# Weight conversions at even distances, their first steps pinned to the order of emission

## The chip, the cores and the metric

The kernel runs on one core of a Trainium2 chip. The time is the device time of one execution in microseconds (us); three executions of the kernel before were timed, and one more was profiled. Engines are called as the profile calls them: PE is TensorE (PEld its weight loads), DVE is VectorE, ACT is ScalarE, POOL is GpSimd, SP is SyncE, whose queue issues all the DMAs here.

## The reference

A block of local and global attention is followed by two feed-forward networks, all in float32:

```python
s_ll = where(|i - j| <= 32, q_l @ k_l.T / 8, -1e9);  s_lg = q_l @ k_g.T / 8
out_l = softmax([s_lg, s_ll]) @ [v_g, v_l];  out_g = softmax(q_g @ [k_g, k_l].T / 8) @ [v_g, v_l]
x = concat(out_g, out_l)                  # 2176 tokens (4 batches of 544), 512 wide
x = relu(x @ w_in) ** 2 @ w_out           # 512 -> 2048 -> 512
out = ((x @ w1) * (x @ w2)) @ w3 @ w_out2 # 512 -> 1024 -> 1024 -> 512
```

## The kernel before

**Products of split numbers.** A float32 factor is held as two parts, `hi` (rounded) and `lo` (the rest), and a product is three matmuls (`PASSES`). Activations are split in tiles named `hl`: ACT rounds (L460, or L471 in `h_unit`), DVE subtracts (L106).

**Weights.** The 72 weight tiles w0 to w71 of 128 x 512 come as 8-byte words and are converted on the chip. `load_w(n)` loads tile `wraw` (512 KB, two buffers). `conv_a(n)`: ACT, two steps (L415, L416). `conv_b(n)`: DVE, two steps (L421, then L424), and the load of w(n+2). `conv_c(n)`: POOL adds (L434), ACT rounds into the final tile (L435), DVE subtracts (L106). The final tiles are named by their pool tag: `va` for w16 to w23, `vb` for w24 to w31, `ub` for w32 to w39, `ua` for w40 to w63, `ub` for w64 to w71. `conv(n)` emits conv_c(n-1), conv_b(n) and conv_a(n+1).

**Stages.** Pass A takes each of eight token blocks (256 or 288 columns) through the first half of the first network, interleaved with the attention; its last two blocks (6 and 7, from about 345 us) run after the attention, as lists of steps made by `rows`: `h_unit` f = 0 to 7 (12 matmuls, relu and squares on ACT L470, L475, L471, a DVE split into `hl`), and `x_add` f (12 matmuls into `acc`), which needs that split. Pass B (from about 398 us) does the same for eight blocks with w16 to w31; x_add f needs w(24+f). In pass B the sixteen `w_unit`s multiply w3 by the last weights (12 matmuls of 512 columns into `wacc`, L652): unit u needs w32 to w39 and w(40+u). Each second unit is copied by ACT to tile `ws` (L658) and stored; `ws` shares the two `wraw` buffers. The last stage (from about 652 us) needs w56 to w71 and the stored products.

**Order.** `merge(main, (steps, lo, hi))` runs the main list and emits the steps of a fill list spread over main steps lo to hi. The framework's scheduler then sets the order on each engine by its own estimate of the times: an instruction that it holds ready is placed ahead of earlier-emitted ones that are not. `tc.keep_in_program_order(ins)` adds one edge: ins stands behind the instruction emitted just before it on the same engine. On the chip each engine keeps the order that is set.

Of the kernel before, what the change touches and what calls it, by code (L numbers as in the profile page):

```python
# [9 lines left out]
F32 = mybir.dt.float32  # L10
# [4 lines left out]
AF = mybir.ActivationFunctionType  # L15
# [49 lines left out]
RUNS = (0, 16, len(UNITS))  # L65
# [10 lines left out]
def attention_mlp(ctx: ExitStack, tc: tile.TileContext, kq0, kq, vw, wts, mask, ident, out):  # L76
    nc = tc.nc
# [329 lines left out]
    def load_w(n):  # L407
        t = pools["cv"].tile([128, 512, 2], I32, tag="wraw", name="wraw", bufs=2)
        nc.sync.dma_start(out=t, in_=wts[n].bitcast(I32).rearrange("p (c w) -> p c w", w=2))
        raw_t[n] = t  # L410

    def conv_a(n):
        raw = raw_t[n]
        t = [pools["cv"].tile([128, 512], I32, tag=f"wt{k}", name="wt", bufs=2) for k in range(3)]
        nc.scalar.activation(t[0].bitcast(F32), raw[:, :, 1].bitcast(F32), AF.Copy, scale=2.0**-112)  # L415
        nc.scalar.activation(t[2], raw[:, :, 0].bitcast(U32), AF.Copy, scale=2.0**-29)  # L416
        mid_t[n] = t

    def conv_b(n):
        raw, (a, b, _) = raw_t.pop(n), mid_t[n]  # L420
        nc.vector.tensor_scalar(  # L421
            out=a, in0=a, scalar1=3, scalar2=0x7FFFFFF8, op0=ALU.logical_shift_left, op1=ALU.bitwise_and
        )
        nc.vector.scalar_tensor_tensor(  # L424
            out=b, in0=raw[:, :, 1], scalar=-(1 << 31), in1=a, op0=ALU.bitwise_and, op1=ALU.bitwise_or
        )
        if n + 1 not in RUNS and n + 2 not in RUNS:
            load_w(n + 2)

    def conv_c(n):  # L430
        _, b, m = mid_t.pop(n)
        tag = UNITS[n]
        t = pools[tag].tile([128, 2, 512], F32R, tag=tag, name=tag, bufs=8)
        nc.gpsimd.tensor_tensor(out=b, in0=b, in1=m, op=ALU.add)  # L434
        nc.scalar.copy(t[:, 0], b.bitcast(F32))  # L435
        split_lo(nc.vector, t[:, 1], b.bitcast(F32), t[:, 0])
        w_t[n] = t

    def conv(n):

        if n in RUNS:
            conv_a(n)
        else:
            conv_c(n - 1)
        conv_b(n)
        if n + 1 in RUNS:
            conv_c(n)
        else:
            conv_a(n + 1)
# [59 lines left out]
    def rows(i, w_in, w_out, split, end):  # L509

        n = block(i)[1]
        steps = []
        for f in range(9):
            if f < 8:
                steps.append(lambda f=f: h_unit(i, f, w_in + f))
            if 4 <= f < 8:
                steps.append(lambda f=f: split(f - 4))
            if f > 0:
                steps.append(lambda f=f: x_add(i, f - 1, w_t[w_out + f - 1], n))
        steps.append(lambda: [end(d) for d in range(4)])  # L520
        return steps
# [5 lines left out]
    def merge(main, *fills):  # L527

        at = [0] * len(fills)
        for n, f in enumerate(main):  # L530
            f()
            for k, (steps, lo, hi) in enumerate(fills):
                upto = min(len(steps), max(0, -(-len(steps) * (n + 1 - lo) // (hi - lo))))
                while at[k] < upto:
                    steps[at[k]]()
                    at[k] += 1
        assert all(a == len(f[0]) for a, f in zip(at, fills))
# [39 lines left out]
    main = [lambda f=f: h_unit(0, f, f) for f in range(8)]  # L577
# [8 lines left out]
    def split_a(i, d):  # L586
        if i < NBLK:
            split_x(i, d, xcols(i)[:, d])
        else:
            split_x(i, d, x_t[0][:, 0, d])  # L590
# [12 lines left out]
    for i in range(0, NBLK, 2):  # L603
        main = []
        for j in (i, i + 1):
            if j >= SHARED:
                main += rows(
                    j, 0, 8, lambda d, j=j: split_a(j + 1, d), lambda d, j=j: end_a(j, d, acc[d])
                )
                continue  # L610
            if j > 0:
                main += [lambda f=f, j=j: h_unit(j, f, f) for f in range(8)]
            main += [lambda d=d, j=j: x_unit_a(j, d) for d in range(4)]
        b = i // 2 + 1
        if b < B:
            if b == 1:
                spill(1)
                load_kq(H // 2)
                for k in range(H, min(H + 3, FIRST_SPLIT)):
                    load_v(k)  # L620
            if b * H == FIRST_SPLIT:
                at_cm.__exit__(None, None, None)
                cv_cm.__exit__(None, None, None)
                at_cm, cv_cm = pool("at2", "right"), pool("sp")
                at, pools["cv"] = at_cm.__enter__(), cv_cm.__enter__()
                for k in range(2):
                    load_v(FIRST_SPLIT + k)
            steps = [s for j in range(4 * b - 1, 4 * b + 4) for s in cycle(j, j < 4 * b + 3, j >= 4 * b)]
            steps.append(lambda i=i: (spill(i + 2), spill(i + 3)))
            fills = [(steps, 0, len(main) - 5)]  # L630
        else:
            for cm in (at_cm, rot_cm, cv_cm):
                cm.__exit__(None, None, None)
            u2 = pools["va"] = pools["vb"] = ctx.enter_context(pool("u2", "right"))
            pools["cv"] = ctx.enter_context(pool("cv2"))
            load_w(16)
            load_w(17)
            main.insert(18, lambda: load_x(0))
            fills = [([lambda n=n: conv(n) for n in range(16, 33)], 0, 31)]
        merge(main, *fills)  # L640


# [2 lines left out]
    def w_unit(f, half):  # L645
        if half == 0:
            wacc[f] = ps.tile([128, 512], F32, tag="x", name="wacc", bufs=X_BUFS)
        o = wacc[f]
        w3 = w_t[40 + 2 * f + half]
        for q in range(4):  # L650
            for k, (a, b) in enumerate(PASSES):
                mm(  # L652
                    o, w3[:, a, 128 * q : 128 * (q + 1)], w_t[32 + 4 * half + q][:, b],
                    start=(half + q + k == 0), stop=(half + q + k == 6),
                )
        if half == 1:
            t = pools["cv"].tile([128, 512], F32, tag="wraw", name="ws", bufs=2)
            nc.scalar.copy(t, o)  # L658
            nc.sync.dma_start(out=w_d[f], in_=t)
# [12 lines left out]
    main = []  # L672
    for i in range(NBLK):
        main += rows(
            NBLK + i, 16, 24, lambda d, i=i: split_b(i + 1, d), lambda d, i=i: end_b(i, d)
        )
    fill = [lambda n=n: conv(n) for n in range(33, 43)]
    for f in range(8):
        fill.append(lambda f=f: w_unit(f, 0))
        fill.append(lambda f=f: w_unit(f, 1))  # L680
        if f < 7:
            fill += [lambda n=n: conv(n) for n in (43 + 2 * f, 44 + 2 * f)]
    fill += [lambda n=n: conv(n) for n in range(57, 72)]
    merge(main, (fill, len(main) // 10, 9 * len(main) // 10))

# [131 lines left out]
```

## Time and profile before

| | us |
|---|---|
| median of 3 executions | 945.86 (944.57 to 948.61) |
| the profiled execution | 945.08 |
| its span, first to last instruction | 943.3 |
| PE busy | 899.1 |
| ACT, DVE, POOL busy | 499.5, 469.6, 321.2 |

PE is the engine with the most work. What a change can give here is read from PE's idle time in the stage concerned, and from what ends it.

### The profile page before, as it was taken

What the parts mean: (1) busy time and instruction counts of PE and PEld (TensorE: products, weight loads), DVE (VectorE), ACT (ScalarE), POOL (GpSimd) and SP (SyncE); (2) the same over time, 40 slices, a digit from 0 to 9 for tenths busy, and PEclk for the clock granted to TensorE, in tenths of its full rate; (3) what the DMA queues carried; (4) which work ended last, traced back from release to release, by engine and by line L of the source; (5) the groups of instructions that cost most, each with busy time, mean ns of one, the idle gap of its engine ahead of it and who ended that gap; (6) DMA issues with size and microseconds to landing.
All of it is one profiled execution on the core that took longest, in us unless ns stands there. A gap on an engine that the chain in (4) does not pass through costs nothing.

```text
span 943.3 us, 16424 instructions
## 1 busy us (share of the span) xinstructions
PE 899.1 (95%) x6064; PEld 822.3 (87%) x6064; DVE 469.6 (50%) x1139; ACT 499.5 (53%) x1291; POOL 321.2 (34%) x354
## 2 busy tenths in 40 slices
PE   7899899799999999988999999999999999999998
PEld 4677798699999989987999999999988888888886
DVE  6984465466867649999354353994110210200201
ACT  6975767657667748887464464884211211211211
POOL 5593452376656824433011121430211111111111
PEclk9999999989999999999999999999999999999999
DMA  8644667665668335656144333654200110100101
GB/s 269 204 148 115 168 156 186 184 142 127 156 188 200 84 108 172 227 178 202 32 157 146 132 112 134 207 192 133 98 23 1 43 42 1 42 1 1 42 1 42
DMA packets 61952, 113.07 MB, mean 120 GB/s; under 512 B 6320, under 2 KB 37168, under 8 KB 61872
## 3 DMA queue, kind: packets, MB, share of 16 engines
q1 hardware_dynamic: 61872, 112.03, 40.3%
q8 instruction: 48, 0.79, 0.3%
q14 instruction: 32, 0.26, 0.1%
HBM read 71.63 MB, written 19.92 MB: 97 GB/s over the span
## 4 chain that ended last, share of the span: by engine, by line
PE 63%; DMA 12%; DVE 10%; ACT 4%; issue 4%; POOL 4%; SPq 3%; DVEq 0%; POOLq 0%; ACTq 0%
PE ab L110 20%; PE acc L504 16%; PE h L110 9%; PE wacc L652 5%; PE x L110 4%; DMA wraw<-in_wts 4%; PE o L339 4%; DMA kq_hl<-kqhi 3%; PE sc L110 2%; DMA kqraw<-in_kq 2%; DVE wt L421 2%; DVE wt L424 2%; PE tp L305 2%; DVE hl L106 2%; POOL wt L434 1%
## 5 line engine op out<-in xcount | busy, mean ns | idle before, releaser
L434 POOL TENSOR_TENSOR wt<-wt 128x512 int32<-128x512 int32 x72 | 101.5, 1409 | 232.8 <-DVE wt L424 158.3
L723 DVE TENSOR_TENSOR r<-r,ab 128x480 f32<-128x480 f32 (+1 forms) x40 | 24.3, 607 | 220.2 <-PE ab L110 219.5
L110 PE MATMUL h<-hl,ua 128*128 128x256 f32 (+1 forms) x768 | 121.3, 303 | 8.5 <-ACT r L470 6.1
L110 PEld LDWEIGHTS h<-hl,ua 128*128 128x128 f32 x768 | 107.7, 200 | 12.4 <-ACT r L470 7.0
L504 PE MATMUL acc<-hl,vb 128*128 128x256 f32 (+1 forms) x768 | 112.9, 290 | 5.2 <-DVE hl L106 4.9
L110 PE MATMUL h<-hl,va 128*128 128x256 f32 (+1 forms) x768 | 112.3, 288 | 1.9 <-DVE hl L106 1.9
L106 POOL TENSOR_TENSOR hl_c<-r,hl_c 128x480 fp32r<-128x480 f32 x32 | 39.2, 1224 | 210.8 <-ACT hl_c L725 203.0
L504 PEld LDWEIGHTS acc<-hl,vb 128*128 128x128 f32 x768 | 103.0, 188 | 9.0 <-DVE hl L106 7.3
L110 PEld LDWEIGHTS h<-hl,va 128*128 128x128 f32 x768 | 102.9, 188 | 3.7 <-DVE hl L106 2.8
L110 PE MATMUL x<-hl,ub 128*128 128x288 f32 (+1 forms) x576 | 88.8, 295 | 3.3 <-POOL hl L106 3.3
L504 PE MATMUL acc<-hl_c,wv 128*128 128x480 f32 x384 | 89.2, 380 | 0.0
L110 PE MATMUL ab<-hl_c,ua 128*128 128x480 f32 x384 | 87.1, 380 | 0.0
L110 PE MATMUL ab<-hl_c,ub 128*128 128x480 f32 x384 | 86.6, 380 | 0.0
L110 PEld LDWEIGHTS ab<-hl_c,ub 128*128 128x128 f32 x384 | 72.0, 188 | 11.9
L722 ACT COPY r<-ab 128x480 f32<-128x480 f32 (+1 forms) x40 | 20.9, 522 | 116.1 <-PE ab L110 113.8
L110 PEld LDWEIGHTS ab<-hl_c,ua 128*128 128x128 f32 x384 | 71.9, 188 | 11.9
L110 PEld LDWEIGHTS x<-hl,ub 128*128 128x128 f32 x576 | 76.8, 189 | 6.1 <-POOL hl L106 4.5
L504 PEld LDWEIGHTS acc<-hl_c,wv 128*128 128x128 f32 x384 | 72.0, 188 | 11.4
L204 ACT ACTIVATE p<-p,st 128x256 f32<-128x256 f32 x128 | 64.2, 504 | 22.5 <-DVE st L200 22.3
L214 POOL TENSOR_TENSOR p<-p,st 128x512 f32<-128x512 f32 x56 | 61.8, 1106 | 35.4 <-DVE st L209 27.6
L470 ACT ACTIVATE r<-h 128x288 f32<-128x288 f32 (+1 forms) x128 | 49.2, 391 | 43.9 <-PE h L110 43.3
L415 ACT ACTIVATE wt<-wraw 128x512 f32<-128x512 f32 x72 | 48.4, 672 | 34.9 <-DMA wraw<-in_wts 32.4
(108 smaller groups left out, 1554.7 us busy)
## 6 DMA issues: line engine op xcount, KB each, us to landing
wraw<-in_wts SPq DMA_DIRECT2D x72, 512.0 KB, 3.4
kq_hl<-kqhi SPq DMA_DIRECT2D x24, 280.0 KB, 3.2
kq_hl<-kqraw SPq DMA_DIRECT2D x48, 136.0 KB, 3.2
vraw<-in_vw SPq DMA_DIRECT2D x16, 256.0 KB, 3.3
x2l<-x_d SPq DMA_DIRECT2D x4, 960.0 KB, 6.0
out<-y SPq DMA_DIRECT2D x16, 240.0 KB, 2.3
kqraw<-in_kq SPq DMA_DIRECT2D x24, 144.0 KB, 2.9
kq_hl<-kqraw SPq DMA_DIRECT2D x24, 144.0 KB, 3.4
```

Source lines behind the costliest of these rows:

```text
L106: eng.tensor_tensor(out=lo, in0=raw, in1=hi.bitcast(F32), op=ALU.subtract)
L110: mm(o, w, x, start=(k == 0), stop=(k == len(terms) - 1))
L204: nc.scalar.activation(p[:, n, :], p[:, n, :], AF.Exp, bias=least[:, n : n + 1], scale=-1.0, accum_out=sums[:, n, 0:1],)
L214: nc.gpsimd.tensor_tensor(out=p, in0=p, in1=over.unsqueeze(2).to_broadcast([128, 2, 256]), op=ALU.mult)
L339: mm(to, w, x, start=(k == 0), stop=(k == len(terms) - 1))
L415: nc.scalar.activation(t[0].bitcast(F32), raw[:, :, 1].bitcast(F32), AF.Copy, scale=2.0**-112)
L434: nc.gpsimd.tensor_tensor(out=b, in0=b, in1=m, op=ALU.add)
L470: nc.scalar.activation(r, h, AF.Relu)
L504: mm(acc[d], w[:, a, 128 * d : 128 * (d + 1)], g_t[f][:, b], start=(f + k == 0), stop=(f + k == 9),)
L652: mm(o, w3[:, a, 128 * q : 128 * (q + 1)], w_t[32 + 4 * half + q][:, b], start=(half + q + k == 0), stop=(half + q + k == 6),)
L722: nc.scalar.copy(r, a)
L723: nc.vector.tensor_tensor(out=r, in0=r, in1=b, op=ALU.mult)
```

## The change

The conversions of w16 to w71 are spread differently, and two of their instructions (L415 and L421 of before) get the edge. In the last main list of pass A there were 17 conversions in 31 of 43 steps, now 14 over all 43. In pass B there were 55 entries from step 16 to 151 of 168, with w_units two by two; now 4 conversions stand in the first 12 steps, and 38 entries from step 12 to 154, of which sixteen hold a conversion and, right behind it, the w_unit that uses the tile before.

```diff
-        nc.scalar.activation(t[0].bitcast(F32), raw[:, :, 1].bitcast(F32), AF.Copy, scale=2.0**-112)
+        first = nc.scalar.activation(t[0].bitcast(F32), raw[:, :, 1].bitcast(F32), AF.Copy, scale=2.0**-112)
+        if n >= RUNS[1]:
+            tc.keep_in_program_order(first)
...
-        nc.vector.tensor_scalar(
+        first = nc.vector.tensor_scalar(
...
+        if n >= RUNS[1]:
+            tc.keep_in_program_order(first)
...
-            fills = [([lambda n=n: conv(n) for n in range(16, 33)], 0, 31)]
+            fills = [([lambda n=n: conv(n) for n in range(16, 30)], 0, len(main))]
...
-    fill = [lambda n=n: conv(n) for n in range(33, 43)]
-    for f in range(8):
-        fill.append(lambda f=f: w_unit(f, 0))
-        fill.append(lambda f=f: w_unit(f, 1))
-        if f < 7:
-            fill += [lambda n=n: conv(n) for n in (43 + 2 * f, 44 + 2 * f)]
-    fill += [lambda n=n: conv(n) for n in range(57, 72)]
-    merge(main, (fill, len(main) // 10, 9 * len(main) // 10))
+    late = [lambda n=n: conv(n) for n in range(30, 34)]
+    fill = [lambda n=n: conv(n) for n in range(34, 72)]
+
+    for u in range(16):
+        fill[u + 7] = lambda u=u: (conv(41 + u), w_unit(u // 2, u % 2))
+    merge(main, (late, 0, 12), (fill, 12, 11 * len(main) // 12))
```

The first place is DVE at the start of the stretch, at the conversions of w16 to w18. In the order of before:

```order
L421 TENSOR_SCALAR wt_4853<-wt_4853 128x512
L424 SCALAR_TENSOR_TENSOR wt_4854<-wraw_4830,wt_4853 128x512
L421 TENSOR_SCALAR wt_4862<-wt_4862 128x512
L424 SCALAR_TENSOR_TENSOR wt_4863<-wraw_4832,wt_4862 128x512
L106 TENSOR_TENSOR hl_4848<-r_4847,hl_4848 128x256
L106 TENSOR_TENSOR va_4886<-wt_4854,va_4886 128x512
L106 TENSOR_TENSOR hl_4881<-r_4880,hl_4881 128x256
L106 TENSOR_TENSOR va_4934<-wt_4863,va_4934 128x512
```

And in the changed kernel, whose lines L423, L428 are L421, L424 of before:

```order
L106 TENSOR_TENSOR hl_4848<-r_4847,hl_4848 128x256
L423 TENSOR_SCALAR wt_4853<-wt_4853 128x512
L428 SCALAR_TENSOR_TENSOR wt_4854<-wraw_4830,wt_4853 128x512
L106 TENSOR_TENSOR hl_4881<-r_4880,hl_4881 128x256
L106 TENSOR_TENSOR hl_4916<-r_4915,hl_4916 128x256
L106 TENSOR_TENSOR va_4921<-wt_4854,va_4921 128x512
L423 TENSOR_SCALAR wt_4862<-wt_4862 128x512
L428 SCALAR_TENSOR_TENSOR wt_4863<-wraw_4832,wt_4862 128x512
L106 TENSOR_TENSOR hl_4960<-r_4959,hl_4960 128x256
L106 TENSOR_TENSOR hl_5009<-xb_3756,hl_5009 128x288
L106 TENSOR_TENSOR hl_5004<-r_5003,hl_5004 128x256
L106 TENSOR_TENSOR va_4977<-wt_4863,va_4977 128x512
```

Before, the first DVE step of a conversion stood ahead of the last one of the conversion before it; now it stands behind it, and the splits of activations (`hl`) stand in between.

The second place is ACT where the same conversions begin. Before:

```order
L415 ACTIVATE wt_4853<-wraw_4830 128x512
L416 ACTIVATE wt_4855<-wraw_4830 128x512
L470 ACTIVATE r_4847<-h_4834 128x256
L415 ACTIVATE wt_4862<-wraw_4832 128x512
L471 ACTIVATE hl_4848<-r_4847 128x256
```

And now (L418 is L416 of before, L474, L475, L479 are L470, L471, L475):

```order
L418 ACTIVATE wt_4855<-wraw_4830 128x512
L474 ACTIVATE r_4847<-h_4834 128x256
L475 ACTIVATE hl_4848<-r_4847 128x256
L479 ACTIVATE r_4847<-r_4847 128x256
L415 ACTIVATE wt_4853<-wraw_4830 128x512
```

Only the pinned step moved behind the first relu; the other one still stands ahead of it.

The third place is PE and ACT among the w_units. Before, PE took the two units of one product in one go, from tiles that DVE had finished well ahead (ua_6563 stands 23 rows before ua_6591 in DVE's order):

```order
L652 MATMUL wacc_6638<-ub_5839,ua_6563 128x512 x3
L652 MATMUL wacc_6638<-ub_5867,ua_6563 128x512 x3
L652 MATMUL wacc_6638<-ub_5901,ua_6563 128x512 x3
L652 MATMUL wacc_6638<-ub_5968,ua_6563 128x512 x3
L504 MATMUL acc_6344<-hl_6558,vb_5407 128x256
L504 MATMUL acc_6348<-hl_6558,vb_5407 128x256
L504 MATMUL acc_6352<-hl_6558,vb_5407 128x256
L504 MATMUL acc_6356<-hl_6558,vb_5407 128x256
L652 MATMUL wacc_6638<-ub_6012,ua_6591 128x512 x3
```

Now a unit comes after each 12 matmuls of the main list, each from the tile that was converted last (L508, L656 are L504, L652 of before):

```order
L656 MATMUL wacc_6545<-ub_5752,ua_6532 128x512 x2
L110 MATMUL h_6826<-hl_6495,va_5071 128x288 x2
L656 MATMUL wacc_6545<-ub_5752,ua_6532 128x512
L656 MATMUL wacc_6545<-ub_5799,ua_6532 128x512 x3
L656 MATMUL wacc_6545<-ub_5846,ua_6532 128x512 x3
L656 MATMUL wacc_6545<-ub_5905,ua_6532 128x512 x3
L110 MATMUL h_6826<-hl_6529,va_5071 128x288 x3
L110 MATMUL h_6826<-hl_6589,va_5071 128x288 x3
L110 MATMUL h_6826<-hl_6651,va_5071 128x288 x3
L508 MATMUL acc_6779<-hl_6809,vb_5423 128x288
L656 MATMUL wacc_6545<-ub_5981,ua_6592 128x512 x2
```

ACT there has the first steps of two conversions, the copy to `ws` (L662, L658 of before) and the rounding (L439, L435 of before) behind each other:

```order
L415 ACTIVATE wt_6475<-wraw_6385 128x512
L418 ACTIVATE wt_6477<-wraw_6385 128x512
L479 ACTIVATE r_6808<-r_6808 128x288
L415 ACTIVATE wt_6540<-wraw_6473 128x512
L418 ACTIVATE wt_6542<-wraw_6473 128x512
L662 COPY ws_6492<-wacc_6392 128x512
L439 CAST ua_6592<-wt_6476 128x512
L474 ACTIVATE r_6839<-h_6826 128x288
L439 CAST ua_6666<-wt_6541 128x512
```

Before, the copy stood ahead of the next conversion's first steps, with the steps of two h_units and no other conversion around it.

## Rows read from the trace of the kernel before

**Rows 1.** Busy time of each engine by stretches, from 345 us on.

```profile
core 0: us, PE busy (x) PEld busy (x) DVE busy (x) ACT busy (x) POOL busy (x), PEclk, DMA share, GB/s
345.00:400.00 55.00, 50.10 (x378) 48.99 (x377) 45.77 (x69) 42.65 (x100) 20.04 (x15) 0.97 0.66 216
400.00:440.00 40.00, 34.20 (x259) 32.20 (x259) 38.49 (x55) 32.63 (x76) 15.79 (x12) 1.00 0.50 167
440.00:580.00 140.00, 140.00 (x969) 132.53 (x968) 66.97 (x120) 75.51 (x173) 22.73 (x17) 1.00 0.41 135
580.00:652.00 72.00, 69.29 (x519) 66.85 (x518) 51.24 (x84) 52.18 (x120) 18.98 (x13) 1.00 0.49 161
652.00:943.30 291.30, 286.97 (x1452) 251.31 (x1452) 45.03 (x76) 57.41 (x111) 45.14 (x40) 1.00 0.09 32
```

**Rows 2.** PE's waits from 345 to 440 us: total, times, longest.

```profile
PE acc L504 <- DVE hl L106: 6.3, 8, 1.4
PE h L110 <- ACT r L470: 2.8, 2, 2.1
PE h L110 <- DVE hl L106: 1.5, 2, 1.0
```

**Rows 3.** PE's largest wait from 580 to 655 us, columns as above.

```profile
PE acc L504 <- DVE hl L106: 1.9, 4, 0.9
```

**Rows 4.** Groups on DVE and POOL, 345 to 440 us: busy, mean ns, idle before.

```profile
L424 DVE SCALAR_TENSOR_TENSOR wt<-wraw,wt 128x512 int32<-128x512 int32 x26 | 18.0, 692 | 0.9
L421 DVE TENSOR_SCALAR wt<-wt 128x512 int32<-128x512 int32 x26 | 13.8, 533 | 9.6 <-ACT wt L415 9.6
L106 DVE TENSOR_TENSOR ub<-wt,ub 128x512 fp32r<-128x512 f32 x8 | 12.8, 1598 | 0.1
...
L434 POOL TENSOR_TENSOR wt<-wt 128x512 int32<-128x512 int32 x26 | 35.8, 1378 | 66.7 <-DVE wt L424 55.8 <-ACT hl L471 4.3 <-ACT r L470 3.0
```

**Rows 5.** Timeline at 372 us: start, duration, engine, line.

```profile
372.70 1.34 POOL L434 TENSOR_TENSOR wt<-wt 128x512 int32<-128x512 int32 x1 [2.12 <-ACT va L435]
...
372.82 1.78 DVE L106 TENSOR_TENSOR va<-wt,va 128x512 fp32r<-128x512 f32 x1
```

**Rows 6.** Timeline of one conversion without overlap, 543.8 to 547.8 us.

```profile
543.80 0.43 DVE L421 TENSOR_SCALAR wt<-wt 128x512 int32<-128x512 int32 x1 [3.41 <-ACT wt L415]
...
544.26 0.69 DVE L424 SCALAR_TENSOR_TENSOR wt<-wraw,wt 128x512 int32<-128x512 int32 x1
...
545.12 1.29 POOL L434 TENSOR_TENSOR wt<-wt 128x512 int32<-128x512 int32 x1 [16.14 <-ACT hl L471]
...
545.58 1.12 DVE L106 TENSOR_TENSOR hl<-r,hl 128x256 fp32r<-128x256 f32 x1 [0.63 <-ACT r L475]
546.45 0.62 ACT L435 CAST ua<-wt 128x512 fp32r<-128x512 f32 x1 [0.90 <-POOL wt L434]
...
547.10 0.69 DVE L106 TENSOR_TENSOR ua<-wt,ua 128x512 fp32r<-128x512 f32 x1 [0.40 <-ACT ua L435]
...
547.71 0.43 DVE L421 TENSOR_SCALAR wt<-wt 128x512 int32<-128x512 int32 x1
```

**Rows 7.** Chain that ended last, 550 to 600 us: start, us, what.

```profile
555.47 1.42 PE acc L504 x12
...
558.31 2.75 PE wacc L652 x12
...
578.59 1.59 PE acc L504 x12
...
586.18 0.60 ACT ws L658
...
586.79 2.01 DMA w_d<-ws
...
588.82 4.06 DMA wraw<-in_wts
```

**Rows 8.** Timeline of ACT, then of PE, 347 to 354 us.

```profile
350.96 0.66 ACT L415 ACTIVATE wt<-wraw 128x512 f32<-128x512 f32 x1 [2.63 <-DMA wraw<-in_wts]
351.52 0.65 ACT L416 ACTIVATE wt<-wraw 128x512 int32<-128x512 uint32 x1
352.08 0.37 ACT L470 ACTIVATE r<-h 128x256 f32<-128x256 f32 x1
352.35 0.69 ACT L415 ACTIVATE wt<-wraw 128x512 f32<-128x512 f32 x1
...
352.50 1.68 PE L110 MATMUL h<-hl,ua 128*128 128x256 f32 x12 [2.13 <-ACT r L470]
```

**Rows 9.** DMA issues, 345 to 652 us: KB each, median us to landing.

```profile
wraw<-in_wts SPq DMA_DIRECT2D x56, 512.0 KB, 3.3
```

## The prediction

> **What bounds the kernel now.** Start with the busy time by stretches [rows 1]: the change touches only what is converted from 345 us on, so what PE loses there is all that can come back. PE is idle for 4.9 us from 345 to 400 us, 5.8 from 400 to 440, none from 440 to 580, 2.7 from 580 to 652: 13.4 us. Behind 652 us no conversion is left, and its 4.3 us are at the end. The granted clock is 1.00 or close to it (0.97 in the first stretch, 1.00 in the others), so no term here is one of clock. Next the waits: of the 10.7 us before 440 us, 7.8 end with a DVE split of an activation and 2.8 with a relu on ACT [rows 2]; the late idle time is mostly DVE again [rows 3].
>
> DVE is what is full there: busy 38.5 of 40 us, but 67 of 140 in the next stretch, where PE never waits [rows 1]. In 95 us it ran 26 conversions [rows 4], one each 3.7 us, ten of them of w32 and later, which no block of tokens needs. The groups show an oddity: the last DVE step of a conversion took 1.6 us on average for `ub` [rows 4], and 1.78 us where it began beside a POOL add [rows 5], against 0.69 us alone [rows 6]. A conversion so takes up to 0.4 + 0.7 + 1.8 = 2.9 us of a queue that also holds the splits PE waits for. The kernel before thus converts in two bursts, each with PE idle, and coasts in between.
>
> **What the change does.** The work is the same: 72 conversions, the same splits and loads. Only places change, so the sum is one of idle time, stretch by stretch.
>
> First the new pace. The pin puts a conversion's first DVE step behind the last DVE step of the one before, so conversions no longer overlap; each costs a full chain: DVE, DVE, POOL, ACT, DVE. The trace holds this chain with nothing in its way: L421 at 543.80, L424, the add at 545.12, the rounding at 546.45, the split at 547.10, the next L421 at 547.71 us [rows 6], 3.9 us. In the changed order 17 other DVE steps of some 0.43 us stand between L421 and L424 in the 40 conversions of w16 to w55, 0.2 us each; and the rounding can find ACT, four fifths busy in the full stretch [rows 1], at another step, for which I add 0.2 to 0.3. I take 4.3 to 4.4 us per conversion; 3.9 is the floor, and 5.3 (the chain plus two whole ACT steps of 0.7) the ceiling.
>
> Against it stands what PE has to do meanwhile. From the first matmul that needs w26 to the first that needs w51, the changed order gives PE 303 matmuls of 256 columns, 360 of 288 and 132 of 512. At 1.42, 1.59 and 2.75 us per 12 [rows 7] these are 35.9 + 47.7 + 30.3 = 113.8 us for 25 conversions, 4.55 each. Among the w_units it is tighter: 12 matmuls of 512 and 12 of 288 per conversion, 4.34 us. So the chain just fits, with little to spare. The gains and losses:
>
> - Start, 2.1 of the 4.9 us. PE waited from 350.4 for a relu that stood behind L415 and L416, both waiting for the first load until 350.96 [rows 8]. Only L415 moves behind it, and L416 still waits for that load; the relu comes one step of 0.56 us earlier. 1.6 stay. (Had both moved, the relu would wait for no load.)
> - The rest to 400 us, 2.8 us. About as many conversions run here as before, but each holds DVE for 1.8 us instead of up to 2.9, since the add of a conversion falls between its own DVE steps. Bounds 0 and 2.8; the steps behind a waiting split still wait with it, so I keep half, 1.4.
> - 400 to 440 us, 5.8 us. Here PE's order asks for w26 to w31 themselves, one per 4.6 us, and the chain gives one per 4.4. Bounds 0 and 5.8; nearer to the first, as the pace fits: 1.5.
> - 440 to 580 us, nothing lost so far. The work taken out of the burst now lies here. What stands against it is the buffer that `ws` shares with `wraw`. For a pair of conversions it goes round: load 3.3 us [rows 9], the second load's first steps some 1.4 behind (two loads issued together fed ACT at 350.96 and 352.35 [rows 8]), 1.1 for those two steps, copy 0.6, store 2.0 [rows 7]: 8.4 us, or 9.2 with the load of 4.06 that stood in the chain [rows 7]. PE has 2 x 4.34 = 8.7 us. Over seven pairs that is 0 to 3.5 us; I take 1.5, and 0.5 for chance encounters between w32 and w39.
> - 580 to 652 us, 2.7 us. The last fifteen conversions had 2.5 blocks of pass B and now have 3, some 5 us each; 1.0 stays, the more so as in the last block DVE now has one split of a stored product ahead of the first activation split. Bounds 0 and 2.7.
>
> The loads move with L424, which issues them, and SP's queue keeps the order loads and stores had; a load has one chain of 3.9 us to land in 3.3, so it stays covered, and the cover is gone if a load takes over 5 us.
>
> Idle after: 1.6 + 1.4 + 1.5 + 2.0 + 1.0 = 7.5 us instead of 13.4. The gain is 5.9 us: 945.08 - 5.9 = 939.2 for the profiled execution, which lies 0.8 under the median shown, so 940.0 for a median.
>
> One row speaks against the change. In the chain alone, the activation split beside the POOL add took 1.12 us instead of some 0.42 [rows 6]. In the new order such splits stand right there, one to three per conversion, where before the conversion's own split took most of the hit. If PE had no slack, 24 conversions (w16 to w39) at 0.7 us would cost 17 us; but in the stretch from 440 to 580, where these rows lie, PE lost nothing with 17 adds [rows 1]. I charge nothing beyond the terms above. The Trainium skill, SBUF — State Buffer, section Who interferes with whom, states the rule: a DVE instruction with two SBUF inputs and a GpSimd instruction that reads SBUF exclude each other, and the second to start waits for the whole of the first. By that rule a split that starts with the add loses its full 1.3 us, and the 24 would cost at most 31 us in all without slack, none with it; the trace agrees with the size (1.78 against 0.69).
>
> **Rivals.**
>
> *Slower: the chain becomes the bound.* If the rounding or a load is late often enough, a conversion takes over 4.55 us, and PE, which now uses each tile right after it is made, waits for each. At 5.2 us: 25 x 0.65 = 16 us, idle 1.6 + 1.4 + 16 + 1.0 = 20 us, 7 more than before, 953. It breaks even at 4.9 us and is slower by over 0.5% from 5.1 on. For it: ACT is about four fifths busy where the pins begin, and no step behind one that waits for a load can pass it. Against it: the bare chain leaves 0.65 us, and conversions that are fewer per microsecond leave ACT freer.
>
> *No change that can be seen: the waits move.* DVE still serves in order, and now a waiting split holds the activation splits behind it, where before a busy one did. If that costs what the fullness cost, PE loses 11 to 14 us as before: 943 to 947. For it: three quarters of the waiting is for splits in that queue [rows 2]. Against it: DVE is busy for 1 us less per conversion.
>
> *All of it comes back.* With conversions spread evenly, DVE would be busy everywhere as it is from 440 to 580 us, where PE lost nothing [rows 1]. Only the first stall stays: 13.4 - 1.6 = 11.8 us, 934. Against it: the pace in the first 60 us hardly falls. The Trainium skill, Perfetto Trace Analysis, section Optimization Strategy, gives this as advice: where the most-contended engine changes over time, interleaving those regimes may improve performance; no run here shows it yet for this kernel.
>
> **How the numbers follow.** The forecast gets 0.52, with a range of its own from 936.5 to 943; the chain as bound 0.17; waits that move 0.18; all back 0.13. A difference of 0.5%, 4.7 us, is about what a measurement of this kernel can tell from none. Four fifths of the forecast's range lie below 941.1: 0.42, and with "all back" 0.55 for faster. Of the chain's 0.17, 0.11 is beyond 950.6. The rest, 0.34, is within. The range from 935.5 to 947 leaves out the far half of "all back" and most of the chain's case, a fifth together.
>
> **What would show it.** Right: L421 at least 3.9 us apart from 350 us on, nowhere a conversion's last split of 1.7 us, DVE below nine tenths from 400 to 440 us, PE idle there under 3 us, and a first stall of 1.6 us at 350 us. Wrong: PE waits on `acc` for `vb` or on `wacc` for `ua`, distances of L421 of 5 us and more between w26 and w56, ACT idle before L415 for loads by more than 2 us at a time, or PE idle from 440 to 580 us above 4 us.

## The result, and the profile after

The changed kernel took 932.71 us (median of four executions), the kernel before 945.23 beside it on the same chip: a ratio of 0.985, 95% interval 0.982 to 0.988. It is faster by 12.5 us where 5.9 were forecast, and lies below the range. One of the four, the profiled one, ran at a granted clock of 0.848 and took 977.42 us, so the ratio is of the other three (median 932.52), and the rows here are of a second set of executions of the same kernel. That set has a median of 934.46 us (ratio 0.989, 0.986 to 0.993); its profiled execution took 933.09, with a span of 931.3.

Busy time by stretches, answering to [rows 1]:

```profile
core 0: us, PE busy (x) PEld busy (x) DVE busy (x) ACT busy (x) POOL busy (x), PEclk, DMA share, GB/s
345.00:400.00 55.00, 53.03 (x426) 52.63 (x424) 29.88 (x59) 38.67 (x93) 12.91 (x10) 1.00 0.52 169
400.00:440.00 40.00, 39.83 (x319) 39.62 (x318) 25.82 (x51) 31.14 (x76) 10.40 (x9) 1.00 0.49 165
440.00:580.00 140.00, 138.69 (x934) 128.90 (x933) 78.53 (x147) 88.85 (x197) 37.88 (x29) 1.00 0.52 174
580.00:652.00 72.00, 71.10 (x561) 70.22 (x560) 45.10 (x87) 49.64 (x118) 13.95 (x12) 1.00 0.47 154
652.00:931.30 279.30, 274.95 (x1353) 239.34 (x1351) 38.14 (x59) 51.96 (x96) 43.20 (x38) 1.00 0.07 24
```

PE's idle time is now 2.0, 0.2, 1.3 and 0.9 us in the four stretches, 4.4 in all instead of 13.4. From 400 to 440 us DVE is busy for 25.8 of 40 us instead of 38.5, and PE does 319 matmuls there instead of 259. PE's waits in the windows 345 to 440, 440 to 580 and 580 to 655 us (total, times, longest), answering to [rows 2, 3]:

```profile
PE h L110 <- ACT r L474: 2.1, 3, 1.6
...
PE acc L508 <- DVE hl L106: 0.9, 2, 0.7
PE h L110 <- ACT r L474: 0.4, 1, 0.4
...
PE h L110 <- ACT r L474: 0.8, 1, 0.8
```

The 7.8 us that ended with a DVE split before 440 us are gone altogether. The groups of 345 to 440 us (busy, mean ns, idle before), answering to [rows 4]:

```profile
L438 POOL TENSOR_TENSOR wt<-wt 128x512 int32<-128x512 int32 x18 | 23.3, 1295 | 75.7 <-DVE wt L428 56.4 <-ACT wt L418 11.6 <-ACT hl L475 4.9
L428 DVE SCALAR_TENSOR_TENSOR wt<-wraw,wt 128x512 int32<-128x512 int32 x19 | 13.1, 688 | 0.4
L423 DVE TENSOR_SCALAR wt<-wt 128x512 int32<-128x512 int32 x19 | 8.0, 420 | 0.1
L106 DVE TENSOR_TENSOR vb<-wt,vb 128x512 fp32r<-128x512 f32 x8 | 5.5, 691 | 4.3 <-ACT vb L439 4.1
```

Nineteen conversions run there instead of 26, and the last split takes 0.69 us each time, not up to 1.78 [rows 5]. The timeline from 348 us shows the first stop and the first conversion, answering to [rows 6, 8]:

```profile
348.73 2.63 PE L110 MATMUL h<-hl,ua 128*128 128x256 f32 x21
...
351.99 0.66 ACT L418 ACTIVATE wt<-wraw 128x512 int32<-128x512 uint32 x1 [2.67 <-DMA wraw<-in_wts]
352.56 0.37 ACT L474 ACTIVATE r<-h 128x256 f32<-128x256 f32 x1
...
352.98 1.68 PE L110 MATMUL h<-hl,ua 128*128 128x256 f32 x12 [1.62 <-ACT r L474]
...
354.41 0.43 DVE L423 TENSOR_SCALAR wt<-wt 128x512 int32<-128x512 int32 x1
...
354.87 0.69 DVE L428 SCALAR_TENSOR_TENSOR wt<-wraw,wt 128x512 int32<-128x512 int32 x1
...
355.73 1.30 POOL L438 TENSOR_TENSOR wt<-wt 128x512 int32<-128x512 int32 x1 [18.30 <-DVE wt L428]
...
357.17 0.62 ACT L439 CAST va<-wt 128x512 fp32r<-128x512 f32 x1
...
357.82 0.69 DVE L106 TENSOR_TENSOR va<-wt,va 128x512 fp32r<-128x512 f32 x1
...
358.43 0.42 DVE L423 TENSOR_SCALAR wt<-wt 128x512 int32<-128x512 int32 x1
```

The first stop lasts 1.62 us, since the relu L474 still stands behind L418, which waits for the first load. A conversion takes 4.0 us and the next begins when its split is done; the add (355.73 to 357.03) meets no last split.

**A stage to compare by.** What lies ahead of 345 us is not touched by the change, and yet the first `h` matmul of block 6 began anywhere from 345.5 to 350.2 us in the profiles that are compared here, though PE, DVE, ACT and POOL have the same instructions in the same order up to there. The runs are therefore also compared by the stage from that matmul to the first `ab` matmul of the last stage. Its busy time before, and in the changed kernel:

```profile
347.74:652.47 304.73, 291.32 (x2103) 278.31 (x2102) 202.33 (x325) 203.23 (x467) 77.54 (x56) 0.99 0.48 159
```

```profile
348.73:640.39 291.66, 287.31 (x2103) 276.02 (x2102) 171.92 (x325) 202.21 (x467) 73.18 (x56) 1.00 0.50 166
```

The columns are those of the first fence. The stage is 13.1 us shorter (the span 12.0, as it began 1.0 later). PE's idle time fell by 9.1 us, from 13.4 to 4.3; the other 4.0 came out of its busy time, 291.3 to 287.3 us for the same matmuls. PE has 957 matmuls of 256 columns, 952 of 288 and 192 of 512 here; at the pace of [rows 7] they need 113.2 + 126.1 + 44.0 = 283 us. So the stage before had lost 21 us and not 13.4.

Part of the 4.0 is clock. The mean of 0.97 in the first stretch of [rows 1] is a granted clock of 0.50 (1.2 GHz) for 3.41 us and of 1.00 (2.4 GHz) for the rest:

```profile
372.17:375.58 3.41, 3.41 (x17) 3.41 (x17) 3.38 (x6) 3.34 (x8) 1.34 (x1) 0.50 0.44 156
```

There 16 matmuls, eight of 256 and eight of 288 columns, took 3.54 us from start to start (372.10 to 375.64), for which the pace of [rows 7] gives 2.0: 1.5 us are lost, and PE counts as busy. In the changed kernel the clock stays at 1.00 for the whole stage. The other 2.5 us lay in stops: the first 0.16 us of each do not show as idle time (the last section), and the stage before has 21 stops that show, the changed one 8.

### The profile page after: what moved, and what is told of

Its sections match the earlier page's. It is cut to its first block, busy times and chain, and to the rows that moved or that the text cites. A ratio compares the mean times of both kernels' runs of the same rounds, so it can differ in the third digit from the quotient of the medians.

```text
span 975.6 us, 16410 instructions
## 1 busy us (share of the span) xinstructions
PE 945.8 (97%) x6064; PEld 853.8 (88%) x6064; DVE 441.0 (45%) x1139; ACT 501.4 (51%) x1291; POOL 315.9 (32%) x354
## 4 chain that ended last, share of the span: by engine, by line
PE 83%; DMA 7%; ACT 3%; DVE 3%; SPq 2%; POOL 2%; issue 1%; DVEq 0%; POOLq 0%; ACTq 0%
PE acc L508 24%; PE ab L110 21%; PE h L110 18%; PE x L110 5%; PE wacc L656 5%; PE o L339 4%; DMA wraw<-in_wts 3%; PE sc L110 2%; PE tp L305 2%; DMA kq_hl<-kqhi 2%; DMA kqraw<-in_kq 1%; DMA vraw<-in_vw 1%; PE sg L110 1%; DVE kqraw L106 1%; SPq L144 1%
## 5 line engine op out<-in xcount | busy, mean ns | idle before, releaser
L438 POOL TENSOR_TENSOR wt<-wt 128x512 int32<-128x512 int32 x72 | 97.0, 1348 | 238.1 <-DVE wt L428 159.2
L110 PE MATMUL h<-hl,va 128*128 128x256 f32 (+1 forms) x768 | 116.8, 299 | 0.1
L508 PE MATMUL acc<-hl,vb 128*128 128x256 f32 (+1 forms) x768 | 116.4, 299 | 0.0
L508 PEld LDWEIGHTS acc<-hl,vb 128*128 128x128 f32 x768 | 108.4, 194 | 1.9
L110 PEld LDWEIGHTS h<-hl,va 128*128 128x128 f32 x768 | 107.9, 195 | 1.8 <-ACT r L474 0.3
L508 PE MATMUL acc<-hl_c,wv 128*128 128x480 f32 x384 | 95.9, 400 | 0.0
L110 PE MATMUL x<-hl,ub 128*128 128x288 f32 (+1 forms) x576 | 93.1, 305 | 2.3 <-POOL hl L106 2.3
L110 PE MATMUL ab<-hl_c,ua 128*128 128x480 f32 x384 | 93.6, 401 | 0.0
L110 PE MATMUL ab<-hl_c,ub 128*128 128x480 f32 x384 | 93.0, 402 | 0.0
L508 PEld LDWEIGHTS acc<-hl_c,wv 128*128 128x128 f32 x384 | 73.3, 191 | 16.8
L110 PEld LDWEIGHTS x<-hl,ub 128*128 128x128 f32 x576 | 81.0, 195 | 4.9 <-POOL hl L106 3.2
L474 ACT ACTIVATE r<-h 128x288 f32<-128x288 f32 (+1 forms) x128 | 49.7, 393 | 56.6 <-PE h L110 52.6
L727 ACT CAST hl_c<-r 128x480 fp32r<-128x480 f32 x32 | 19.0, 593 | 90.5 <-DVE r L725 90.5
```

The costliest lines, as they stand in the source:

```text
L110: mm(o, w, x, start=(k == 0), stop=(k == len(terms) - 1))
L474: nc.scalar.activation(r, h, AF.Relu)
L508: mm(acc[d], w[:, a, 128 * d : 128 * (d + 1)], g_t[f][:, b], start=(f + k == 0), stop=(f + k == 9),)
```

## The experiments

Stage lengths are from the profiled execution of each, one per kernel, so differences of 1 to 2 us between them rest on single executions; the two sets of the changed kernel alone differ by 1.9 us in median. The ratio is to the kernel before on the same chip. Pace is the mean distance of the first 28 starts of a conversion's first DVE step (L421 before); the last column is how long the granted clock was 0.50 within the stage.

| kernel | median us (range) | ratio [95%] | stage us | pace us | half clock us |
|---|---|---|---|---|---|
| before | 944.95 to 946.67 in four sets | | 304.7 | 3.42 | 3.41 |
| changed, second set | 934.46 (933.09 to 938.24) | 0.989 [0.986, 0.993] | 291.7 | 4.61 | 0 |
| distances without pins | 940.59 (939.49 to 942.51) | 0.994 [0.992, 0.996] | 301.2 | 3.48 | 3.41 |
| both pins alone | 928.96 (927.89 to 932.95) | 0.983 [0.980, 0.986] | 288.4 | 4.59 | 0 |
| distances, DVE pin | 937.37 (933.92 to 939.09) | 0.991 [0.988, 0.994] | 297.8 | 4.66 | 3.41 |
| pins, new pace, old w_units | 931.19 (930.62 to 936.03) | 0.985 [0.983, 0.988] | 290.2 | 4.60 | 3.41 |
| pins, old pace, interleaved w_units | 934.14 (929.58 to 935.70) | 0.987 [0.984, 0.989] | 293.2 | 4.62 | 0 |
| DVE pin alone | 936.06 (932.93 to 938.35) | 0.988 [0.986, 0.991] | 292.9 | 4.66 | 3.41 |
| pins, add on DVE | 932.72 (930.83 to 936.94) | 0.987 [0.984, 0.989] | 290.6 | 4.27 | 0 |
| no pin, add on DVE | 935.84 (933.42 to 939.41) | 0.989 [0.986, 0.992] | 295.9 | 3.40 | 3.41 |
| three pins | 929.05 (928.85 to 929.33) | 0.982 [0.980, 0.983] | 287.1 | 4.62 | 0 |
| changed, longer chain | 974.36 (971.97 to 977.22) | 1.029 [1.026, 1.032] | 305.9 | 5.98 | 10.24 |
| changed, own buffer for `ws` | 929.22 (928.03 to 930.58) | 0.983 [0.980, 0.985] | 289.9 | 4.61 | 0 |

**The parts of the change.** Theory A: the pins do it, since the last split of a conversion no longer runs beside the add of the next one. Theory B: the even distances do it. The changed kernel again, with no edit:

> The changed kernel once more, for a profile at full clock. Theory A (the pin): a conversion's own steps on VectorE no longer meet its POOL add, so VectorE spends some 1.8 us on one instead of 2.6, the queue has room, and TensorE loses nothing behind the first stall: 931 to 933 us, TensorE idle under 3 us from 345 to 652 us, no conversion split of over 1 us. Theory B (the pace): the idle time went because fewer conversions run before 440 us; VectorE's cost of one stays as it was, above 2.4 us. The step of the prediction under test is its terms 1.4, 1.5, 2.0 and 1.0 us, all expected near zero now.

The distances without the pins, with these lines gone at both places:

```diff
-        if n >= RUNS[1]:
-            tc.keep_in_program_order(first)
```

> The new distances without the two pins. In its order 37 of 55 conversions still start on VectorE ahead of the last step of the one before, as 39 did before the change, and the weights w24 to w40 stand within five places of where they stood. Theory A: the gain is nearly gone, 941 to 945 us, with splits of 1.7 us beside the adds. Theory B, by which the even distances do it: 933 to 936 us.

The pins on the old distances (the last hunks of the change undone):

```diff
+            fills = [([lambda n=n: conv(n) for n in range(16, 33)], 0, 31)]
...
+    merge(main, (fill, len(main) // 10, 9 * len(main) // 10))
```

> The kernel before with the two pins, old distances. No conversion starts on VectorE ahead of the last step of the one before. Theory A: most of the 10.7 us before 440 us come back, 933 to 937 us, and what the old crowding at the end costs stays (up to 2.7 us from 580 to 652 us). Theory B: 941 to 945 us.

The new distances with DVE's pin alone, the edge gone at L415 only:

```diff
         first = nc.scalar.activation(t[0].bitcast(F32), raw[:, :, 1].bitcast(F32), AF.Copy, scale=2.0**-112)
-        if n >= RUNS[1]:
-            tc.keep_in_program_order(first)
         nc.scalar.activation(t[2], raw[:, :, 0].bitcast(U32), AF.Copy, scale=2.0**-29)
```

> The new distances with the pin on VectorE alone. Theory A: 931 to 933.5 us, as with both, since the pin on VectorE alone takes the overlap away. If the pin on ScalarE matters (the first relu no longer behind one of two steps that wait for a load), 0.5 to 2 us more than with both: 933 to 935 us.

The pins are the change: 17.6 us alone, against 5.9 for the distances alone and 12.1 for both. Theory A named the right part, but several of its ranges were missed: the pins alone came out 4 us better than its range, the changed kernel again 1.5 us above it, and DVE's pin with the new distances 3.9 us above it. Without pins PE's waits are what they were, here from 345 to 650 us with the new distances:

```profile
PE acc L504 <- DVE hl L106: 8.1, 10, 1.4
PE h L110 <- ACT r L470: 2.3, 2, 2.1
```

With the pins and the old distances they are:

```profile
PE h L110 <- ACT r L474: 3.1, 3, 1.6
PE acc L508 <- DVE hl L106: 0.8, 1, 0.8
```

The reason stands in DVE's order. Before, 39 of 55 conversions began on DVE ahead of the last split of the one before, with the distances alone 37, with DVE's pin none. The pins, not the new places, also set the pace: with the old places and both pins conversions start 4.59 us apart, nineteen of them before 440 us, as in the changed kernel, and DVE is as free (columns as in the first fence); with the new places and no pin they start 3.48 us apart, 26 of them before 440 us.

```profile
400.00:440.00 40.00, 40.00 (x322) 40.00 (x321) 26.94 (x52) 30.30 (x74) 11.68 (x9) 1.00 0.52 168
```

So the pins change two things at once, the meeting and the pace, and these runs do not separate them; the runs with the add on DVE below do. With the new distances and no pin on ACT, PE meets a new wait, for the rounding L437 (L435 of before) in the w_units L654:

```profile
PE wacc L654 <- ACT ua L437: 3.1, 2, 1.8
PE acc L506 <- ACT hl L473: 1.4, 2, 1.2
```

DVE's pin alone, on the old distances (to the kernel before):

```diff
+        if n >= RUNS[1]:
+            tc.keep_in_program_order(first)
         nc.vector.scalar_tensor_tensor(
```

> The kernel before with the pin on VectorE's first step alone, old distances. Theory A (what counts is that the last split of a conversion no longer runs beside the add of the next one, which VectorE's pin alone brings about): 928 to 933 us, splits of 0.69 us. Rival (ScalarE's pin has an equal share): 936 to 941 us, with PE stops on the rounding of a conversion or on a relu. In either case the first stall at 350 us stays at 2.1 us or more.

By its stage, DVE's pin is worth 11.8 of the 16.3 us, ACT's the other 4.5: the rival with equal shares gave the right median, but part of that was a start of the stage at 350.2 us. Of the 4.5 some 1.5 us are clock: without ACT's pin the first stop is 2.1 us, and the granted clock fell to 0.50 for 3.41 us 1.6 us behind it. With the new distances the shares are the other way round: 3.4 us for DVE's pin (301.2 to 297.8), 6.1 for ACT's (297.8 to 291.7). PE's waits on ACT here are 3.3 us for relus, the first stop in them, and 0.8 for the rounding of an activation; there is none for the rounding of a conversion.

**What the new distances cost under the pins.** The changed kernel's stage is 3.2 us longer than that of the pins alone. Two halves were tried apart; first the new places with the w_units two by two as before, then the old ranges with each w_unit behind a conversion:

```diff
-    fill = [lambda n=n: conv(n) for n in range(34, 72)]
...
-    for u in range(16):
-        fill[u + 7] = lambda u=u: (conv(41 + u), w_unit(u // 2, u % 2))
+    fill = [lambda n=n: conv(n) for n in range(34, 43)]
+    for f in range(8):
+        fill.append(lambda f=f: w_unit(f, 0))
+        fill.append(lambda f=f: w_unit(f, 1))
...
```

> Both pins and the new distances of the plain conversions, but the w_units two by two with two conversions between pairs, as in the kernel before. In the profiles so far PE needs 304.7 us from the first matmul of block 6 to the first matmul of the last stage in the kernel before, 291.7 in the changed one and 288.4 with the pins alone. Theory I (the w_unit right behind its conversion is what costs the changed kernel its 3 to 5 us): 928 to 931 us, stretch 288 to 289.5. Theory P (the slower first list and the later fill cost them): 933 to 936 us, stretch 291 to 292.

```diff
+            fills = [([lambda n=n: conv(n) for n in range(16, 33)], 0, 31)]
...
+    fill = [lambda n=n: conv(n) for n in range(33, 72)]
...
+        fill[u + 8] = lambda u=u: (conv(41 + u), w_unit(u // 2, u % 2))
+    merge(main, (fill, len(main) // 10, 9 * len(main) // 10))
```

> Both pins, the old first list (17 conversions in 31 steps) and the old range of the fill (16 to 151), but each w_unit right behind a conversion. Theory I: 932 to 936 us, with PE stops on relu and hl from about 530 to 620 us. Theory P: 928 to 931 us.

The stage is 4.8 us longer than that of the pins alone with the interleaving and 1.8 with the new places; in medians the two lie 5 and 2 us above the pins alone, at the edge of what can be told apart. Some 1.4 of the 1.8 us are clock: the granted clock was 0.50 for 3.41 us from 510.58 us, behind one stop of 1.9 us that ended with a DVE split. So theory I has the better of it, though the run with the new places lies just above its ranges (931.19 and 290.2 us against at most 931 and 289.5), and the two costs do not add up to the 3.2. The chain that ended last in the changed kernel shows one such place (start, us, what):

```profile
542.67 0.61 DVE wt L428
...
543.30 4.37 DMA wraw<-in_wts
...
547.70 0.67 ACT wt L415
...
548.39 0.44 DVE wt L423
...
548.85 0.69 DVE wt L428
549.55 0.35 DVE hl L106
...
549.94 1.21 PE acc L508 x8
```

A load issued behind a conversion's L428 took 4.37 us, where 3.3 is the median before [rows 9]; the next conversion and the activation split behind it came later, and PE stopped for 0.7 us. It ran beside the store of `ws`, which landed at 544.87 us, and the next load of a weight, which was issued as that store landed, at 544.88; which of its neighbours made it long is not shown. The loop through the buffers was then opened by giving `ws` its own:

```diff
-            t = pools["cv"].tile([128, 512], F32, tag="wraw", name="ws", bufs=2)
+            t = pools["cv"].tile([128, 512], F32, tag="wst", name="ws", bufs=1)
```

> The changed kernel with a buffer of its own for ws, so that the loads no longer wait for its copy and store. In the changed kernel ScalarE waits 18 times for a load from 440 to 600 us, 20.7 us in all, and PE stops of 0.7 to 1.0 us stand behind such waits. Theory W (that loop is what the interleaved w_units cost): the waits for loads fall under 8 us, PE needs 289.5 to 290.5 us for the stage instead of 291.7, and the time is 930 to 932.5 us. Rival (the steps of a conversion and of a w_unit simply crowd ScalarE and VectorE at one moment): the stage stays at 291 to 292.5 us and the time at 932.5 to 935.

The stage became 1.7 us shorter, as theory W has it, but its reason did not come out: ACT's waits for loads from 440 to 600 us rose, from 20.7 us to 29.9, where it had them under 8. PE's idle time did not fall either, 4.3 us before and 4.4 now (all of it for relus, where 0.9 had been for DVE splits); the 1.7 us lie in what idle time does not show. That the loop cost them is therefore not shown. The median is 5.2 us lower, of which 3.3 lie ahead of the stage (it began at 345.5 us) and are not the edit's.

**The meeting or the order.** The pins do two things: the last split no longer meets an add, and conversions no longer run ahead, so that they come at a slower pace. The integer add was moved to DVE, with the pins and without (the profile shows it there as an operation on 16-bit halves, 0.69 us):

```diff
-        nc.gpsimd.tensor_tensor(out=b, in0=b, in1=m, op=ALU.add)
+        add = nc.vector if n >= RUNS[1] else nc.gpsimd
+        add.tensor_tensor(out=b, in0=b, in1=m, op=ALU.add)
```

> Both pins, old distances, and the integer add of the conversions of w16 to w71 on VectorE and not on GpSimd (its sum is rounded differently there, so the weights are not exact). No add of GpSimd is left for a split to meet, and the chain gets shorter by some 0.6 us, but each conversion holds VectorE for 0.69 us more: 39 us over 56. Theory A (VectorE's time is what PE waited for; the pins gave back 28 us of it): the gain goes back, 940 to 947 us. Rival (the serial order is what helps, by itself, whatever VectorE is busy with): 927 to 932 us.

> The kernel before (no pin, old distances) with the integer add of w16 to w71 on VectorE (rounded differently there, so the weights are not exact). In VectorE's order 34 of 55 conversions still begin ahead of the last split of the one before; before it was 39. No split can meet an add of GpSimd any more. With the run that has the pins and this add it makes a square of two by two. Theory A (the meeting of split and add is what cost): most of the gain comes without a pin, 930 to 937 us. Theory O (the serial order costs less by itself, because conversions no longer run ahead of the splits that PE waits for): 941 to 949 us, with PE stops on hl from 350 to 440 us as before.

With the pins, DVE was busy for 201.5 us from 345 to 652 us, as much as before the change (202.5, from [rows 1]), and yet the stage took 290.6 us: theory A, put as DVE's total busy time, falls. (The median lies 0.7 us above the rival's range.) Without pins the stage took 295.9 us and the median lies where theory A had it. PE's waits from 345 to 650 us, and the busy time in a stretch at half clock and from 400 to 440 us (columns as in the first fence):

```profile
PE h L110 <- ACT r L471: 7.2, 7, 2.3
PE acc L505 <- ACT hl L472: 1.1, 1, 1.1
```

```profile
353.57:356.98 3.41, 3.37 (x15) 3.37 (x16) 3.24 (x7) 2.87 (x8) 0.00 (x0) 0.50 0.93 332
...
400.00:440.00 40.00, 37.97 (x302) 37.41 (x301) 36.46 (x74) 35.91 (x87) 0.00 (x0) 1.00 0.57 188
```

No wait on a DVE split is left, though 34 of 55 conversions still begin ahead, they come 3.40 us apart as before, and DVE is busy for 36.5 of 40 us. So neither a full DVE nor the pace by itself made PE wait for DVE; the steps of up to 1.8 us ahead of an activation split, in place of 0.69, did. What is left is waits on ACT, 2.3 us of them the first stop. So the square reads: 304.7 before, 295.9 without the meeting, 290.6 without the meeting and in order, 288.4 in order with the add back on POOL. If the add on DVE costs 2.2 us in either order, taking the meeting away gave 11.0 us and the order 5.3, together the 16.3 of the pins. Of the 5.3, some 1.5 us are clock (0.50 for 3.41 us in both kernels of the square without pins, in neither with them) and 0.6 the shorter first stop; how the rest divides between order and pace is open. (Without adds on POOL no activation split meets one either; in the changed kernel 24 still do, and PE waits little for them. The chain is shorter too, which this does not separate; but PE waited for no weight before.)

**The first stop.** The same edge for ACT's second step, with the old distances:

```diff
+        if n >= RUNS[1]:
+            tc.keep_in_program_order(second)
```

> Old distances, both pins, and the same edge for ScalarE's second step, so that no step of a conversion stands ahead of the first relu of block 6 and waits there for the first load. The stop at 350 us, 1.5 to 1.6 us in every run with both pins, goes to 0.3 us or less. If nothing else moves: 927 to 928.5 us, against 928.96 with two pins. Rival (the second step, now held in order, makes the next conversion late): 929 to 933 us, with PE stops on relu elsewhere.

The stop is gone; PE runs 33 matmuls where it broke off after 21:

```profile
348.73 4.05 PE L110 MATMUL h<-hl,ua 128*128 128x256 f32 x33
```

The stage is 1.3 us shorter than with two pins. The median, 0.5 us above what was expected if nothing else moved, is that of two pins, as the stage began 1.2 us later in the profile; 1.3 us can't be told in medians here. This kernel, two pins alone and the changed one with its own `ws` buffer are the fastest, and not told apart.

**The rival in which the chain is the bound.** The changed kernel with a longer chain:

```diff
-        nc.gpsimd.tensor_tensor(out=b, in0=b, in1=m, op=ALU.add)
+        if n >= RUNS[1]:
+            nc.gpsimd.tensor_tensor(out=m, in0=b, in1=m, op=ALU.add)
+            nc.gpsimd.tensor_copy(b, m)
...
```

> The changed kernel with one more step in each chain of w16 to w71: GpSimd adds into the third tile and then copies it back, which is exact and gives VectorE and ScalarE nothing to do. The chain of a conversion (4.6 us on average in the changed kernel) gets longer by the copy, some 0.8 to 1.4 us. If the chain is then the bound, as the prediction's rival has it (25 conversions between w26 and w51, PE's work 4.55 us each): at 5.4 us 21 us are lost, at 6.0 us 36, so 950 to 970 us, with PE waits on acc for vb and on wacc for ua. If tiles made ahead, and longer gaps between conversions, take up a longer chain: 933 to 940 us.

The copy took 0.67 us, but the starts of L423 came 5.98 us apart over the first 28 conversions (353.88 to 515.38) instead of 4.61 (354.41 to 478.83). That is 1.37 us more for a step of 0.67; where the rest comes from is not shown. PE's waits from 345 to 655 us, and then the one behind:

```profile
PE acc L512 <- ACT vb L443: 10.9, 5, 2.8
PE h L110 <- ACT r L478: 3.5, 4, 1.8
...
PE ab L110 <- ACT r L728: 26.2, 1, 26.2
```

The span is 42.4 us longer (973.7 against 931.3); the rival's rule gives 25 x (5.98 - 4.55) = 36. The sizes agree partly by luck: only 14.2 us of it are in the stage, and there the granted clock was 0.50 for 10.24 us behind stops of up to 2.9 us, where the changed kernel has 1.00. The most is one wait in the last stage, for a copy on ACT (L728) that stands behind steps of the last conversions, which now come late. At 4.61 us per conversion PE waits for no weight at all. So the rival was a real one, and its threshold lies between 4.61 and 5.98.

## Why the prediction was wrong

The two effects of the pin that the prediction names were seen: conversions no longer overlap, and each costs one chain. The direction was right for that reason. What failed is the size of what can come back; and the sum took pins and places as one, where the pins did the work. In its order:

- **What can come back: the step that failed.** "What PE loses there is all that can come back" took 13.4 us, the idle time of the profile. Against the pace of [rows 7] the stage had lost 21 us. The forecast itself used that pace for PE's need, but not for what PE was losing. "No term here is one of clock" failed with it: the 0.97 that it read hides 3.41 us at 0.50, 1.5 us of PE's time. Of the 7.2 us by which the stage beat the 5.9 forecast, 4.0 come from here: those 1.5, and 2.5 in stops that do not show as idle time.
- **The terms of idle time** add up to 4.4 instead of 7.5 us, the other 3.1. Start: 1.6 forecast, 1.62 measured. The rest to 400 us: 1.4, measured 0.4 (2.0 less the first stop). 400 to 440: 1.5, measured 0.2. 440 to 580: 2.0, measured 1.3. 580 to 652: 1.0, measured 0.9. The two that were mis-sized most are those in which DVE's queue before was fullest: 1.4 was kept for splits that wait behind a conversion's split and 1.5 for the pace, and either cost nearly nothing.
- **Pins and places.** "Only places change" made one sum of both. The new places without pins kept the pace (3.48 us against 3.42) and the waits on DVE, and gave 5.9 us; the pins alone gave 17.6, at the pace of the changed kernel. On top of the pins the new places took 3.2 us of the stage back.
- **The pace.** 4.3 to 4.4 us per conversion were taken, 4.61 were measured, against PE's 4.55. By the rival's rule that is 25 x 0.06 = 1.5 us of waiting for weights; there was none. The first `vb` split begins at 396.2 us and the first matmul that needs it at 403.2, and that lead covers the difference.
- **The loop through `ws`**: the term was 2.0 with the chance encounters, against 1.3 us idle. Opening the loop gave 1.7 us of the stage, but ACT then waited longer for loads, so the mechanism behind the term is not shown.
- **Activation splits beside the add** were charged nothing. Before, 21 began within an add in this stage, after 24; so nothing was to be paid. By the Trainium skill, SBUF — State Buffer, section Who interferes with whom, the second of the two waits for the whole of the first: the last splits agree, with 1.78 us beside an add before [rows 5] and 0.69 in all 56 now.
- **The rivals.** "All of it comes back", 934 us with a chance of 0.13, is nearest in time (933.1 profiled), though 4.4 us of idle time stayed. Its reason, spreading, is not what did it, and with 21 us lost before there was more than "all" to come back: that it is near is luck. "The waits move" fell: a waiting split cost nothing where a busy one had cost.

Of the signs for right, all came: starts of L423 (L421 before) at least 3.9 us apart, no last split over 0.7 us, DVE at 25.8 of 40 us, PE idle there for 0.2, a first stop of 1.62. Of the signs for wrong, two came, and yet PE waited for no weight: nine of the thirty distances from w26 to w56 were over 5 us (the longest 437.76 to 444.96), and ACT sat idle before L415 for a load by up to 5.3 us.

## What to carry to other kernels

Count what an engine loses against its bare pace (start to start, times the number of instructions), not by its idle time alone, and look at what a mean clock below 1.00 is made of: here the 0.97 was 3.41 us at half clock, and they came back too. Where a scheduler may start the next item of a multi-engine pipeline early, look at what its steps then meet on the engine that the critical work waits for; one ordering edge can be worth more than a better spacing of the items. And try the parts of a change alone: here one of them took back some 3 us of what the other gave, and the even pace that the places were meant to bring came from the other.

## What the runs showed of the hardware

A matmul of 256 columns is recorded for some 0.28 us, and the next begins 0.118 us later (1.42 us per 12). A stop so shows as idle time only beyond 0.16 us: the first stop of the changed kernel, 1.62 us in the profile, cost 352.98 - 348.73 - 21 x 0.118 = 1.77 us, and shorter ones don't show at all.

Of the 56 last splits before, 36 overlapped a POOL add. The 23 that began within the add took 1.55 to 1.80 us instead of 0.69, and each ended 0.55 us behind the add, though they began from 0.08 to 0.33 us into it. The other 13 began 0.25 us ahead of the add and took their 0.68 us; there the add took 1.58 to 1.61 us instead of 1.3. The four groups of last splits fell from 63.0 to 38.7 us of busy time from 345 to 652 us.

TensorE's granted clock fell from 1.00 to 0.50 (2.4 to 1.2 GHz) for 3.41 us in the stage of all five kernels without ACT's pin. In four of them the first stop was 2.05 to 2.28 us, and the clock fell within 1.6 us of its end; in the kernel before, with a first stop of 2.13 us, it fell only at 372.17 us, behind stops of 0.69 and 0.87 us. Behind the first stops of the kernels with both pins, at most 1.79 us, it stayed at 1.00; in two of these eight it fell later, behind a stop of 1.9 us and, with the longer chain, stops of up to 2.9 us. At 0.50 a matmul of 256 columns began each 0.214 us, at 1.00 each 0.118.
